# A chunked state-space scan with a gated feed-forward behind it: block 1 in the order of the later blocks, pair 4 prepared in block 0, the last output in two halves, other dummies

## Chip, cores and metric

The kernel runs on one core of one Trainium2 chip. The metric is the device time of one execution in microseconds (us). Three executions of the kernel before took 128.85, 129.83 and 133.45 us; the median is 129.83.

A core has these engines: PE (TensorE, with its weight loads shown apart as PEld), DVE (VectorE), ACT (ScalarE), POOL (GpSimd) and SP (SyncE, which here only issues DMAs). Each engine works through its own queue in order, and they meet at semaphores.

## What is computed

```python
# x [4, 8, 768, 32], a [4, 8, 768], B and C [4, 8, 768, 16]
for c in range(nc):                       # chunks of 32 tokens
    cum = np.cumsum(log_a[chunk])
    L = np.exp(cum_i - cum_j) * causal
    M = (C_c @ B_c.T) * L
    y[chunk] = M @ x_c + (C_c @ state) * np.exp(cum)
    state = np.exp(sum(log_a)) * state + sum_j B_j x_j * np.exp(cum_end - cum_j)
t = y.transpose(0, 2, 1, 3).reshape(3072, 256)
out = (np.maximum(t @ w_gate, 0) * (t @ w_val)) @ w_out   # w_gate, w_val [256, 1536], w_out [1536, 256]
```

## The kernel before

**Tiling.** The scan uses chunks of 128 tokens instead of 32. Two chunks (256 tokens) of all 8 heads are a pair; there are 12 pairs, 3 to each of the 4 batches. Pairs 0 to 3 (`NWIDE`) have B and C loaded with two neighbouring tokens side by side in a partition, the others token by token. The decays are folded into B and C: C is multiplied and B divided by the running product of `a`, so that what is left is a masked C B^T. The feed-forward runs in 6 blocks of 512 tokens, two pairs each. The output of the scan, `yT` (256 features by tokens, bf16), is its input.

**Steps of a pair.** `load` brings B, C and x in by SP's queue (`held` does the same behind a tiny DVE memset, which keeps the DMAs from starting earlier). `scale` is `scale_bc` (two multiplications that give the scaled B and C, the tile `bs`) and `to_x` (x to bf16, the tile `xb`), on POOL for the pairs from 2 on. `turn` transposes B and C on PE; `tevac` copies them out (ACT and DVE). `G` is the masked product's eight matmuls; `gevac` brings them to `gs` with the mask: one and a half of four quarters by ACT with two selects on POOL behind it (`causal`, L168), the rest by DVE. `states` (`state` for the first batch) adds to the running state in PSUM, `spread` (`sevac`) copies it to `Sm` on DVE. `inter` (state times C) and `Dm` (`gs` times x) write the bank `y`, and `yevac` copies it to `yT`: in two strided copies for pairs 0 to 3, in one for the others.

**Steps of a block b.** For each of 12 slices f of 128 hidden features, `gv` makes gate and value for all 512 tokens: two matmuls of 512 columns each (L526, L529), a Relu on ACT (L532) and a product on DVE (L533). `gvh` does the same for half the tokens (256 columns; L544, L551, L552). `fout` makes 128 tokens of output with 12 matmuls of 256 columns (L564), and `foevac` copies and stores: for two groups at a time on ACT and SP; in the last block one at a time, by ACT and ACT's DMA queue for even groups, by DVE and SP's queue for odd ones.

**The order.** `in_order` ties every engine to the order in which the program names its instructions, so the order is written by hand. In block b the names are P = 2b + 2 and Q = 2b + 3, the two pairs of the next block, and W = 2b + 1, the second pair of this block. The first `nh` slices are done in halves: first the half whose `yT` comes from pair 2b, then, when W's `yT` is there, the other. `nh` is 4 in block 0 (whose first halves stand ahead of the loop), 6 in block 1 and 5 after that. W's `inter` and `Dm` come after f == 4 in block 1, after f == 2 in the later blocks. In the later blocks `states(P)` follows them directly; in block 1 it comes behind `fout(1, 0)`. The prologue, up to L689, works through pairs 0 and 1; `keep_warm(n, cols)` puts n matmuls without use (dummies, tile `w`, L200) into PE's queue there.

PSUM has five shared banks (`bank`) that rotate through gate, value, `o` and `g`, and one bank each for `y`, the transposes and the state.

Of the kernel before, what the change touches and what calls it, by code (L numbers as in the profile page):

```python
# [8 lines left out]
FP32 = mybir.dt.float32  # L9
# [20 lines left out]
def kernel(  # L30
# [13 lines left out]
    nc = tc.nc  # L44

    NB, NH, S, D = x.shape
# [5 lines left out]
    NF = DF // 128  # L52
# [13 lines left out]
    def bank(name="bank", shape=(128, 512), dtype=FP32):  # L66
        return mm.tile(list(shape), dtype, tag="shared", bufs=NSHARED, name=name)
# [129 lines left out]
    def keep_warm(n, cols=512):  # L197
        w = mm.tile([128, 512], FP32, tag="y", name="w")
        for _ in range(n):
            nc.tensor.matmul(out=w[:, 0:cols], lhsT=warm[:, 0:128], rhs=warm[:, 0:cols],  # L200
                             start=True, stop=True)
# [73 lines left out]
    def scale_bc(p, eng, js=slice(0, 2), f=None):  # L275
        b, c0, _ = place(p)
        src, dst = views(p, js)
        if f is None:
            if p < NWIDE:
                f = wfac[:, p, js].rearrange("s j r h -> s (j r) h")  # L280
            else:
                f = fac[:, b, c0:c0 + 2].rearrange("s c j h -> s (c j) h")
        n = f.shape[1]
        for t in range(2):
            eng.tensor_tensor(  # L285
                out=dst[:, :, t], in0=src[:, :, t],
                in1=f[:, :, 4 * t:4 * t + 4].to_broadcast([128, n, 4, N]), op=ALU.mult)

    def to_x(p, eng, f=None):
        xb = att.tile([128, 2 * NH * D], BF16, tag="xb", name="xb", bufs=6)  # L290
        xr = st[p]["xr"].rearrange("s i h d -> s (i h) d")
        out = xb.rearrange("s (k d) -> s k d", d=D)
        if f is None:
            copy(eng, out, xr)
        else:
            eng.tensor_tensor(out=out, in0=xr, in1=f.to_broadcast([128, 2 * NH, D]),
                              op=ALU.mult)
        st[p]["x"] = [xb[:, i * NH * D:(i + 1) * NH * D] for i in range(2)]

    def scale(p, eng):  # L300
        new_bs(p)
        scale_bc(p, eng)
        to_x(p, eng)
# [65 lines left out]
    def G(p):  # L369
        s = st[p]  # L370
        if "gp" not in s:
            G_banks(p)
        g = s["gp"]
        for i in range(2):
            for q in range(4):
                r = slice(32 * q, 32 * q + 32)
                nc.tensor.matmul(  # L377
                    out=split(p, g[q][:, i]), lhsT=s["BT"][r, i], rhs=ct(p, i, r),
                    start=(i == 0), stop=True, tile_position=(32 * q, 0),
                    skip_group_check=True)  # L380
        s["gs"] = att.tile([128, 4, 4, 128], BF16, tag="gs", name="gs", bufs=2)
# [51 lines left out]
    def states(p):  # L433
        c0 = 2 * (p % PPB)
        last = c0 + 2 == NC
        chunks[p] = (st[p]["B"], st[p]["x"])
        todo = [(0, p, 0)]
        if c0:
            todo.insert(0, (0, p - 1, 1))
        if not last:  # L440
            todo += [(1, p, 0), (1, p, 1)]
        for n, (k, e, i) in enumerate(todo):
            B_, x_ = chunks[e]
            xi = x_[i].rearrange("s (t q d) -> s q t d", t=2, q=4)
            for q in range(4):
                nc.tensor.matmul(  # L446
                    out=A_ps[0][32 * q:32 * q + 32, 0, 64 * k:64 * k + 64].rearrange(
                        "p (t d) -> p t d", t=2),
                    lhsT=B_[i][:, 32 * q:32 * q + 32], rhs=xi[:, q],
                    start=(n == 0 and c0 == 0), stop=True, tile_position=(0, 32 * q),  # L450
                    skip_group_check=True)

    def spread(p):
        for k in range(1 if 2 * (p % PPB) + 2 == NC else 2):
            S[2 * p + k + 1] = n = att.tile([128, 2, 128], BF16, tag="Sm", name="Sm", bufs=5)
            a = A_ps[0][:, 0, 64 * k:64 * k + 64].rearrange("p (t o d) -> p t o d", t=2, o=1)
            nc.vector.tensor_tensor(  # L457
                out=n.rearrange("p t (q d) -> p t q d", q=4),
                in0=a.to_broadcast([128, 2, 4, D]),
                in1=smask.rearrange("p t (q d) -> p t q d", q=4), op=ALU.mult)  # L460
# [58 lines left out]
    fst = {}  # L519
# [39 lines left out]
    def fout(b, ts):  # L559
# [3 lines left out]
        for f in range(NF):  # L563
# [2 lines left out]
                rhs=wo[:, f], start=(f == 0), stop=(f == NF - 1),  # L566
                skip_group_check=True)

    def foevac(b, ts):
        last = b == NBLK - 1  # L570
        if ts % 2 == 0 and not last:
            return
        ob = ffn.tile([128, 2, DM], FP32, tag="ob", name="ob", bufs=3)
        r0 = b * 512 + ts * 128
        if last:
            i = ts % 2
            (nc.vector.tensor_copy if i else nc.scalar.copy)(out=ob[:, i], in_=fst["o"][:, i])
            (nc.sync if i else nc.scalar).dma_start(out=out[r0:r0 + 128, :], in_=ob[:, i])
            return
        nc.scalar.copy(out=ob, in_=fst["o"])  # L580
        nc.sync.dma_start(
            out=out[r0 - 128:r0 + 128, :].rearrange("(i p) m -> p i m", p=128), in_=ob)
# [9 lines left out]
    nc.vector.reciprocal(r0, d0)  # L592
    scale_bc(0, nc.vector, B_, r0)
    transp(0, 1, True)
    keep_warm(4, 128)
    transp(0, 0, True)
    cevac(0, nc.scalar)
    bevac(0, nc.vector)
# [3 lines left out]
    nc.vector.reciprocal(wfac[:, 1, 0], d1)  # L602
    new_bs(1)
    scale_bc(1, nc.vector, C_)
    G(0)
    gevac(0)

# [18 lines left out]
    keep_warm(3)  # L626
    astep(0, 0)
    sevac(0, 0)
    keep_warm(9, 128)
    scale_bc(1, nc.gpsimd, B_)  # L630
    cast_x(1, (1,))
    weights(4, 8, (1,))
# [58 lines left out]
    for b in range(NBLK):  # L691
        P, Q, W = 2 * b + 2, 2 * b + 3, 2 * b + 1
        more = P < NPAIR
        for n in (P + 2, P + 3):
            if b and n < NPAIR:
                load(n, nc.sync)

        nh = (4, 6, 5)[min(b, 2)]
        for f in range(nh):
            if b == 0:  # L700
                continue
            gvh(b, f, 0)
            if b and f == (4 if b == 1 else 2):
                inter(W, 0)
                inter(W, 1)
                Dm(W)
                if b > 1 and more:
                    states(P)
                yevac(W, nc.scalar)
                if b > 1 and more:  # L710
                    spread(P)
        for f in range(nh):
            gvh(b, f, 1)
            if b == 1 and f in (0, 3):
                scale(P if f == 0 else Q, nc.gpsimd)
        for f in range(nh, NF):
            gv(b, f)
            if b == 0:
                if f == 5:
                    turn(P)  # L720
                    tevac(P, nc.scalar, nc.vector)
                    scale_bc(Q, nc.gpsimd)
                if f == 7:
                    back(P)
                    backevac(P, nc.vector)
                if f == 8:
                    held(Q, bc=False)
                    held(Q + 1)
                if f == 9:
                    state(P, 0)  # L730
                if f == 10:
                    state(P, 1)
                    held(Q + 2)
                    turn(Q)
                    tevac(Q, nc.scalar, nc.vector)
            elif more:
                if f == (6 if b == 1 else 5):
                    turn(P)
                    tevac(P, nc.scalar, nc.vector)
                    if b > 1:  # L740
                        scale(Q, nc.gpsimd)
                if f == (9 if b == 1 else 8):
                    turn(Q)
                    tevac(Q, nc.scalar, nc.vector)
                    if Q + 1 < NPAIR:
                        scale(Q + 1, nc.gpsimd)
        if more and b != 1:
            inter(P, 0)
            inter(P, 1)
        fout(b, 0)  # L750
        foevac(b, 0)
        if b == 1:
            states(P)
        if more:
            G(P)
        if b == 1:
            spread(P)
        if more:
            gevac(P)
        if b == 0:  # L760
            to_x(Q, nc.gpsimd)
            back(Q)
            backevac(Q, nc.vector)
        fout(b, 1)
        foevac(b, 1)
        if b == 0:
            for n in range(NB):
                nc.vector.reciprocal(fac[:, n, :, 0], fac[:, n, :, 1])
        fout(b, 2)
        foevac(b, 2)  # L770
        if more:
            if b == 1:
                inter(P, 0)
                inter(P, 1)
            Dm(P)
            states(Q)
            yevac(P, nc.scalar)
            G(Q)
            spread(Q)
            gevac(Q)  # L780
        fout(b, 3)
        foevac(b, 3)

    in_order(tc)

# [29 lines left out]
```

## Time and profile before

| | |
|---|---|
| runs shown | 128.85, 129.83, 133.45 us (median 129.83) |
| profiled execution | 128.56 us |
| its span, first to last instruction | 126.9 us |
| mean granted clock of PE | 0.986 |
| DMA | 11.72 MB; under 512 B: 66912 of 73136 packets |

| engine | busiest groups (line: count, mean ns of one) |
|---|---|
| PE | L564 `o`: 288, 273; L526 and L529 `gate`, `val`: 84 each, 379; L544 `gv`: 240, 273 |
| PEld | L564: 288, 98 |
| DVE | L533 `h`: 42, 686; L552 `h`: 60, 421; L398 `gs`: 24, 684 |
| ACT | L532 `r`: 42, 597; L551 `r`: 60, 385; L389 `gs`: 12, 590 |
| POOL | L285 `bs`: 16, 620; L168 `gs`: 12 of 644 and 12 of 409; L259 `xb`: 9, 609 |

The mean of one matmul has its way through the array in it and overlaps with its neighbours; in the chain of waits, where each counts from start to start, one of 256 columns takes 0.109 us and one of 512 takes 0.216. "Released by" and idle times are inferred from semaphores.

### The profile page before, as it was taken

To read this page: it belongs to the slowest core of one execution; us is meant where nothing else is said; L and a number is where in the kernel's file an instruction comes from. 1 tells how busy PE (TensorE), PEld (TensorE's weight loads), DVE (VectorE), ACT (ScalarE), POOL (GpSimd) and SP (SyncE) were. 2 spreads that over 40 slices of the span, in tenths; PEclk is the share of its full clock that TensorE was granted. 3 is DMA by queue.
4 is the path that set the end of the run, shared out by engine and by line. 5 is a ranking of instruction groups with operands and counts; after the bars stand their busy time and mean duration, and the time that the engine had idled before them with its cause. 6 is when DMAs were issued, how large, how long until landed. Compare 5 with 4: busy or idle time off the path is not lost.

```text
span 126.9 us, 3376 instructions
## 1 busy us (share of the span) xinstructions
PE 120.6 (95%) x1261; PEld 83.5 (66%) x1261; DVE 93.5 (74%) x225; ACT 78.1 (62%) x173; POOL 42.4 (33%) x79
## 2 busy tenths in 40 slices
PE   6789999999999999999999999999999999999980
PEld 2337784568876568884577875577874678854860
DVE  5686988869969875898865888865898756787420
ACT  4062677644888734888745787635987446877310
POOL 7959696005651313703112803132600033000000
PEclk9967999999999999999999999999999999999999
DMA  3999999979998987099742288822200002200031
GB/s 65 145 184 184 154 204 144 156 109 107 103 178 151 122 88 154 33 121 121 75 71 83 90 79 118 97 47 83 83 5 0 0 0 88 83 0 0 5 123 42
DMA packets 73136, 11.72 MB, mean 92 GB/s; under 512 B 66912, under 2 KB 73120, under 8 KB 73120
## 3 DMA queue, kind: packets, MB, share of 16 engines
q1 hardware_dynamic: 61328, 8.23, 42.0%
q0 software_dynamic: 9424, 2.75, 20.8%
q10 hardware_dynamic: 2368, 0.52, 2.2%
q8 instruction: 10, 0.16, 0.5%
q14 instruction: 6, 0.05, 0.1%
HBM read 11.11 MB, written 3.15 MB: 112 GB/s over the span
## 4 chain that ended last, share of the span: by engine, by line
PE 91%; DVE 3%; DMA 2%; issue 1%; ACT 0%; DVEq 0%
PE o L564 26%; PE gv L544 22%; PE val L529 14%; PE gate L526 14%; PE g L377 3%; PE y L500 3%; DMA a_sb<-in_a_dram 2%; PE y L489 2%; PE tp L317 2%; PE w L200 2%; PE d L222 1%; DVE cp L207 1%; PE A_ps L446 1%; PE bt L358 1%; DVE bs L285 1%; PE A_ps L240 1%
## 5 line engine op out<-in xcount | busy, mean ns | idle before, releaser
L564 PE MATMUL o<-wo,h 128*128 128x256 bf16 x288 | 34.1, 273 | 0.0
L533 DVE TENSOR_TENSOR h<-r,val 128x512 bf16<-128x512 bf16 x42 | 28.8, 686 | 5.4 <-ACT r L532 2.2
L564 PEld LDWEIGHTS <-h 128*128 128x128 bf16 x288 | 27.2, 98 | 5.4 <-issue 1.9
L532 ACT ACTIVATE r<-gate 128x512 bf16<-128x512 f32 x42 | 25.1, 597 | 8.0 <-PE gate L526 7.1
L552 DVE TENSOR_TENSOR h<-r,gv 128x256 bf16<-128x256 bf16 x60 | 24.9, 421 | 5.5 <-ACT r L551 4.8
L168 POOL TENSOR_SCALAR_AFFINE_SELECT gs<-gs 128x512 bf16<-128x512 bf16 (+1 forms) x24 | 12.1, 527 | 46.7 <-ACT gs L389 46.7
L551 ACT ACTIVATE r<-gv 128x256 bf16<-128x256 f32 x60 | 23.1, 385 | 3.3 <-PE gv L544 0.9
L526 PE MATMUL gate<-yT,wg 128*128 128x512 bf16 x84 | 25.0, 379 | 0.0
L529 PE MATMUL val<-yT,wv 128*128 128x512 bf16 x84 | 25.0, 379 | 0.0
L544 PE MATMUL gv<-yT,wg 128*128 128x256 bf16 x120 | 23.1, 273 | 0.2
L544 PE MATMUL gv<-yT,wv 128*128 128x256 bf16 x120 | 22.9, 273 | 0.0
L398 DVE TENSOR_TENSOR gs<-g,masks 128x512 bf16<-128x512 f32 x24 | 15.4, 684 | 4.3 <-PE g L377 4.2
L529 PEld LDWEIGHTS <-wv 128*128 128x128 bf16 x84 | 8.2, 98 | 9.9
L285 POOL TENSOR_TENSOR bs<-bcr,fac 128x256 bf16<-128x256 f32 x16 | 9.6, 620 | 13.4 <-DMA bcr<-in_B_dram 13.4
L389 ACT CAST gs<-g 128x512 bf16<-128x512 f32 x12 | 7.1, 590 | 9.6 <-PE g L377 9.6
L259 ACT CAST yT<-y 128x512 bf16<-128x512 f32 (+1 forms) x14 | 7.1, 528 | 9.3 <-PE y L500 3.6
L544 PEld LDWEIGHTS <-wv 128*128 128x128 bf16 x120 | 11.7, 98 | 1.6 <-issue 0.2
L544 PEld LDWEIGHTS <-wg 128*128 128x128 bf16 x120 | 11.2, 98 | 2.1 <-issue 0.4
L526 PEld LDWEIGHTS <-wg 128*128 128x128 bf16 x84 | 7.8, 98 | 5.9
L457 DVE TENSOR_TENSOR Sm<-A_ps,smask 128x256 bf16<-128x256 f32 x15 | 5.8, 419 | 6.6 <-PE A_ps L446 6.5
L580 ACT COPY ob<-o 128x512 f32<-128x512 f32 x10 | 5.8, 585 | 4.8 <-PE o L564 4.8
L200 PE MATMUL w<-warm 128*128 128x128 bf16 (+1 forms) x30 | 6.7, 380 | 1.3 <-DVE first L118 1.3
(79 smaller groups left out, 104.5 us busy)
## 6 DMA issues: line engine op xcount, KB each, us to landing
out_dram<-ob SPq DMA_DIRECT2D x10, 256.0 KB, 2.2
xr<-in_x_dram SPq DMA_DIRECT2D x18, 128.0 KB, 3.3
bcr<-in_C_dram SPq DMA_DIRECT2D x16, 64.0 KB, 3.0
bcr<-in_B_dram SPq DMA_DIRECT2D x16, 64.0 KB, 3.0
wg<-in_moe_w_gate_dram POOLq DMA_DIRECT2D x3, 256.0 KB, 5.5
wv<-in_moe_w_val_dram POOLq DMA_DIRECT2D x3, 256.0 KB, 5.6
wo<-in_moe_w_out_dram POOLq DMA_DIRECT2D x1, 768.0 KB, 8.5
bcr<-in_B_dram SPq DMA_DIRECT2D x4, 128.0 KB, 4.6
```

Of the source, the lines that this page charges most:

```text
L168: nc.gpsimd.affine_select(out=dst, in_=dst, pattern=pattern, compare_op=ALU.is_ge, fill=0.0, base=0, channel_multiplier=-1)
L200: nc.tensor.matmul(out=w[:, 0:cols], lhsT=warm[:, 0:128], rhs=warm[:, 0:cols], start=True, stop=True)
L285: eng.tensor_tensor(out=dst[:, :, t], in0=src[:, :, t], in1=f[:, :, 4 * t:4 * t + 4].to_broadcast([128, n, 4, N]), op=ALU.mult)
L398: nc.vector.tensor_tensor(out=d[:, q], in0=g[q], in1=m, op=ALU.mult)
L526: nc.tensor.matmul(out=g, lhsT=wg[:, k, fs], rhs=yT[:, k, tk], start=(k == 0), stop=(k == 1))
L529: nc.tensor.matmul(out=v, lhsT=wv[:, k, fs], rhs=yT[:, k, tk], start=(k == 0), stop=(k == 1))
L532: nc.scalar.activation(r, g, AF.Relu)
L533: nc.vector.tensor_tensor(out=fst[b][:, f], in0=r, in1=v, op=ALU.mult)
L544: nc.tensor.matmul(out=gv_[:, j], lhsT=w[:, k, fs], rhs=yT[:, k, tk], start=(k == 0), stop=(k == 1), skip_group_check=True)
L551: nc.scalar.activation(r, gv_[:, 0], AF.Relu)
L552: nc.vector.tensor_tensor(out=fst[b][:, f, u * 256:(u + 1) * 256], in0=r, in1=gv_[:, 1], op=ALU.mult)
L564: nc.tensor.matmul(out=o[:, ts % 2], lhsT=fst[b][:, f, ts * 128:(ts + 1) * 128], rhs=wo[:, f], start=(f == 0), stop=(f == NF - 1), skip_gr ...
```

## The change

Block 1 takes the order of the later blocks: five slices in halves, W after f == 2, `states(P)` and `spread(P)` behind W, the turns at f == 5 and f == 8, `inter(P)` ahead of `fout(1, 0)`. For that, pair 4 (Q + 1 of block 0) is scaled in block 0: `scale_bc` on POOL ahead of pair 3's selects, `to_x` behind them, the loads one slice earlier, the reciprocals of the decays earlier and without the first batch, which nothing reads. The last 128 tokens of output are made by `fout_last` in two column halves, the first copied and stored by ACT, the second by DVE and SP. Dummies: 5 instead of 4 between the two transposes of pair 0, two new ones ahead of `G(0)`, 6 instead of 9 ahead of `Dm(0)`.

```diff
+    def fout_last(b):
+
+        r0 = b * 512 + 384
+        for m in range(2):
+            ms = slice(m * 128, (m + 1) * 128)
+            o = bank("o", (128, 128))
+            for f in range(NF):
+                nc.tensor.matmul(out=o, lhsT=fst[b][:, f, 384:512], rhs=wo[:, f, ms],
+                                 start=(f == 0), stop=(f == NF - 1))
+            ob = ffn.tile([128, 128], FP32, tag="obl", name="ob", bufs=2)
+            (nc.vector.tensor_copy if m else nc.scalar.copy)(out=ob, in_=o)
+            (nc.sync if m else nc.scalar).dma_start(out=out[r0:r0 + 128, ms], in_=ob)
...
     transp(0, 1, True)
-    keep_warm(4, 128)
+    keep_warm(5, 128)
     transp(0, 0, True)
...
     scale_bc(1, nc.vector, C_)
+    keep_warm(2, 128)
     G(0)
...
     sevac(0, 0)
-    keep_warm(9, 128)
+    keep_warm(6, 128)
     scale_bc(1, nc.gpsimd, B_)
...
-        nh = (4, 6, 5)[min(b, 2)]
+        nh = 5 if b else 4
         for f in range(nh):
             if b == 0:
                 continue
             gvh(b, f, 0)
-            if b and f == (4 if b == 1 else 2):
+            if f == 2:
                 inter(W, 0)
                 inter(W, 1)
                 Dm(W)
-                if b > 1 and more:
+                if more:
                     states(P)
                 yevac(W, nc.scalar)
-                if b > 1 and more:
+                if more:
                     spread(P)
         for f in range(nh):
             gvh(b, f, 1)
-            if b == 1 and f in (0, 3):
-                scale(P if f == 0 else Q, nc.gpsimd)
         for f in range(nh, NF):
             gv(b, f)
...
                     backevac(P, nc.vector)
-                if f == 8:
                     held(Q, bc=False)
                     held(Q + 1)
...
             elif more:
-                if f == (6 if b == 1 else 5):
+                if f == 5:
                     turn(P)
                     tevac(P, nc.scalar, nc.vector)
-                    if b > 1:
-                        scale(Q, nc.gpsimd)
-                if f == (9 if b == 1 else 8):
+                    scale(Q, nc.gpsimd)
+                if f == 8:
                     turn(Q)
                     tevac(Q, nc.scalar, nc.vector)
                     if Q + 1 < NPAIR:
                         scale(Q + 1, nc.gpsimd)
-        if more and b != 1:
+        if more:
             inter(P, 0)
             inter(P, 1)
         fout(b, 0)
         foevac(b, 0)
-        if b == 1:
-            states(P)
+        if b == 0:
+            for n in range(1, NB):
+                nc.vector.reciprocal(fac[:, n, :, 0], fac[:, n, :, 1])
         if more:
             G(P)
-        if b == 1:
-            spread(P)
-        if more:
             gevac(P)
         if b == 0:
             to_x(Q, nc.gpsimd)
+            new_bs(Q + 1)
+            scale_bc(Q + 1, nc.gpsimd)
             back(Q)
             backevac(Q, nc.vector)
         fout(b, 1)
         foevac(b, 1)
-        if b == 0:
-            for n in range(NB):
-                nc.vector.reciprocal(fac[:, n, :, 0], fac[:, n, :, 1])
         fout(b, 2)
         foevac(b, 2)
         if more:
-            if b == 1:
-                inter(P, 0)
-                inter(P, 1)
             Dm(P)
             states(Q)
             yevac(P, nc.scalar)
             G(Q)
             spread(Q)
             gevac(Q)
-        fout(b, 3)
-        foevac(b, 3)
+            if b == 0:
+                to_x(Q + 1, nc.gpsimd)
+            fout(b, 3)
+            foevac(b, 3)
+        else:
+            fout_last(b)
```

## The prediction

> **What bounds the kernel now.** I read the page first, then the chain of waits in order of time, then busy time and clock by stretch, and last the timelines of POOL and SP.
>
> ```profile
> span 126.9 us, 3376 instructions
> ...
> PE 120.6 (95%) x1261; PEld 83.5 (66%) x1261; DVE 93.5 (74%) x225; ACT 78.1 (62%) x173; POOL 42.4 (33%) x79
> ...
> PEclk9967999999999999999999999999999999999999
> ```
>
> TensorE is busy for 95% of the span, and after the first quarter of a slice row its digits are all 9: from 8.6 us to 123.3 us the chain of waits runs almost wholly on PE. So work on another engine matters only where it makes PE wait, and there are few such places. PEclk shows one weak stretch, slices 3 and 4. The chain of waits there (start, length, what):
>
> ```profile
> 6.85 0.30 PE tpb L317 x2
> 7.17 0.44 DVE BT L259
> 7.66 0.61 PE g L377 x8
> ...
> 8.60 1.28 PE w L200 x3
> 9.88 0.21 PE A_ps L415
> 10.09 0.91 PE w L200 x9
> 11.04 0.41 PE y L500 x16
> ...
> 11.65 0.45 ACT yT L259
> ```
>
> The reader sees dummies (w, L200) on the path: three wide ones cost 1.28 us, 0.43 each, though 512 columns take 0.216 in the later stages (gate L526, 0.43 for two). The clock is half. Busy time by stretch, cut at steps of 3.41 us (the last columns are clock, DMA share, GB/s):
>
> ```profile
> 3.97:7.38 3.41, 2.40 (x33) 1.43 (x30) 2.40 (x9) 0.84 (x2) 3.33 (x7) 1.00 2.04 141
> 7.38:10.79 3.41, 3.24 (x27) 1.75 (x24) 2.87 (x10) 1.31 (x4) 2.00 (x6) 0.50 1.56 190
> 10.79:14.20 3.41, 3.21 (x49) 2.18 (x46) 2.28 (x7) 1.81 (x5) 2.22 (x3) 1.00 1.41 152
> ```
>
> The granted clock is 0.50 for exactly one stretch of 3.41 us, after a stretch with PE busy for 2.40 of 3.41. Block 1 in the chain of waits:
>
> ```profile
> 33.30 2.18 PE gv L544 x20
> 35.48 0.11 PE y L489 x2
> 35.59 0.34 PE y L500 x16
> 35.93 0.54 PE gv L544 x4
> ...
> 36.48 0.27 PE gv L544
> ...
> 36.79 2.67 PE gv L544 x23
> 39.46 0.43 PE gate L526 x2
> ```
>
> Here 48 narrow matmuls should take 48 x 0.109 = 5.24 (12 take 1.31 at 52.05), with 0.45 for the two y groups 5.69; they take 39.46 - 33.30 = 6.16. PE stalls for 0.47 us. The same count for block 2 (52.05 to 57.17: 40 x 0.109 + 0.22 + 0.34 + 0.09 = 5.01 of 5.12) leaves 0.11. The end:
>
> ```profile
> 118.01 5.25 PE o L564 x48
> ...
> 123.34 0.42 DVE ob L577
> ```
>
> **The change part by part.**
>
> *Dummies.* Three narrow ones less before Dm(0). At half clock one takes 0.107 (0.91 for nine is a mix: half clock to 10.79, then 0.055). Six take 6 x 0.107 = 0.64, so Dm(0) can start 0.27 earlier, at 10.77. What is late next: its gs are done at 9.99 (POOL) and 10.06 (DVE), Sm for inter at 10.56, so nothing holds it. One dummy more at 6.5 lies in PE's idle 0.19 before 6.85, where PE waits for DVE's bs; without that cover it costs 0.06. The two before G(0) lie in the idle 0.17 before 7.66, where PE waits for DVE's BT. They take 0.11 at full and 0.21 at half clock, so 0 to 0.04 sticks out, 0.21 if BT were early. I take -0.24; bounds -0.31 and 0.
>
> *Block 0.* Two memsets of 0.06 move one step up on DVE, from 24.37 to 23.65, into the slack before the next h; SP's x load for pair 3 and all loads for pair 4 go out 0.7 earlier, and pair 5's behind them. Three reciprocals (four took 1.38, so 1.04) move ahead of gs(2) into DVE's idle 1.00 before 28.39; gs(2) may end 0.05 later, at 30.06, and Dm(2) runs at 31.13, so the price is nothing, and without that idle 1.04 would eat all but 0.1 of this margin. The fourth is gone. POOL gets scale_bc(4) (two, 1.20) ahead of gevac(3)'s two selects, and to_x(4) (0.61) behind them. Queued behind scale_bc(4) is Dm(3), through the selects. B(4)'s second half is issued at about 28.5 - 0.7 = 27.7 and loads of that stretch land in 2.9 to 3.4, so it lands by 31.2. POOL is free from to_x(3) at 30.6; scaling ends at 32.4, the selects start at 32.8 as now, to_x(4) ends at 34.4. It is wanted by states(4) after Dm(3), at about 35.0. Zero, with 0.4 to spare on the one and 0.6 on the other.
>
> *Block 1.* Six half steps per side become five: eight narrow matmuls become four wide ones, 8 x 0.109 against 4 x 0.216, nothing. Dm(3) runs after three half steps, at 33.30 + 1.31 + 0.11 = 34.7; gs(3) ends at 33.83 on POOL and 33.93 on DVE. ACT then copies yT in two pieces (0.76, at 35.98 now) while PE has states(4) 0.09 and two half steps 0.87 to do; now it has only one, and there it stalls. So the stall should shrink to block 2's 0.11; but block 2's yT copy is 0.59, so 0.17 may remain on top. Gain 0.19 to 0.36, I take 0.33. POOL's scale(5), now placed after turn(4), still starts when its load lands (36.30, 38.80 in the trace) and is wanted by turn(5) beyond 42: nothing. The inter and states moved over from the end of the block are the same instructions on PE.
>
> *Last output.* Twelve matmuls of 256 columns (1.31) become 24 of 128, each with its own weight load. No long run of this kind is in the trace. The nearest rows: four transposes with four weight loads 0.22, four inter matmuls 0.22, so 0.055 each, 1.32 in all: nothing. The far bound is the mean weight load of 98 ns: 24 x 0.098 = 2.35, 1.04 worse. I take the row of four, as there too each matmul has a fresh weight. A page speaks against this part: the Trainium skill, "TensorE: Matmul & The Clock Gate", section "Back-to-back issue gap", gives about 81 ns per matmul for a stream of load and matmul at 128 columns; by that estimate the 24 would take 1.94, 0.6 more. The groups of four here disagree with it. After PE, DVE copies 128 columns instead of 256: 0.42 becomes 0.29 by the 128x128 products on DVE (L285), and the last DMA is half as large; its 128 KB moved in about 0.5 us. But the first half leaves on ACT's queue right behind the DMA of 122.38, and lands 2.3 after its issue at about 123.05, 125.35, where SP's 1.7 now gives 123.80 + 1.7 = 125.5. So -0.15 to -0.35; I take -0.2.
>
> Sum: -0.24 - 0.33 - 0.2 = -0.77 against the profiled 128.56, whose span is 126.9 with 1.66 around it: 127.8. The three runs shown (128.85, 129.83, 133.45) all lie above it; the two lower ones by 0.78 on average. So I expect **128.5** as the median, 1.0% under 129.83.
>
> **The rivals.**
>
> *The clock stays whole (25%).* If the added dummies lift the stretch before 7.38 over what the gate asks, the half-clock stretch goes. G(0) then takes 0.34 (as at 13.18) instead of 0.61, DVE's gs end at 9.8 and Sm at 10.3, and inter ends at 10.4 instead of 11.63: 1.2 earlier, 0.95 beyond my sum. What may take it back is wo: issued at 17.64, 8.5 to landing, so in place at 26.14, and wanted at 26.49. If it does not move, only 0.35 of the shift survives. 0.1 to 0.95 more gain: 127.5 to 128.4 on the median, 126.8 with a lucky one. For: the gate changed at a step of 3.41 us, and three dummies are added ahead or at its edge. Against: one of them adds 0.06 to 2.40.
>
> *The gate closes later (11%, the slower one).* With three dummies fewer, or with the earlier stretch at full clock and thus sooner done, PE waits more in 7.38 to 10.79, and the half clock falls on 10.79 to 14.20, where PE is busy for 3.21 of 3.41 with real work. That costs half of it, 1.6: 130.1, slower than before. It decides when that stretch's busy time falls toward the 2.40 that closed the gate; by my sum it stays above 3.0, which speaks against it. Two such stretches would give 131.7. The Trainium skill, the same page, section "Part 1: The HAM clock gate", lets the clock fall only after an idle window of about 3.4 us; by that this rival could not happen. The trace agrees on the length, 3.41, but the stretch before the fall was busy for 2.40, so I leave the rival its chance.
>
> *POOL holds block 1 back (6%).* If B(4) lands after 34.7 - 1.03 - 1.20 = 32.5, 4.8 after its issue, PE waits at Dm(3). With the longest landing of the run from such loads, 7.4, scaling ends at 36.3, the selects at 37.3: 2.6 lost, and the 0.33: 131.4. Against: 2.9 to 3.4 in that stretch.
>
> *The last 24 matmuls go at the pace of weight loads (8%).* With 98 ns for each, +1.04: 129.5, no gain that shows. For: no run of more than six in the trace. Against: the groups of four, and six dummies at 5.48 whose six weight loads span 0.34. (The Trainium skill's 81 ns, from the page and section named above, would give 129.1.)
>
> *It does not do what it says (13%).* The stall of block 1 is carried by ACT's backlog, not the order, and the dummies' time reappears as a wait for gs: only the tail is left, 129.3.
>
> **How the numbers follow.** The forecast as worked out has 37%, its own range 127.6 to 129.3. A difference under 2% (2.6 us) cannot be told from none in these runs. Below 127.2 lie part of the whole-clock case and the forecast with a lucky median: 0.6 x 25% + 0.2 x 37% = 22%. Above 132.4 lie two half-clock stretches or a run like 133.45: 8%. The range 126.7 to 130.2 takes in all cases but the POOL one and the tails.
>
> **What would show it.** Right: Dm(0) near 10.8; block 1's half steps in 5.1 + 0.1 with Dm(3) at 34.4 to 34.7; POOL's scale_bc(4) before 32.5 and no wait of PE on gs or bs; 24 last matmuls in 1.3, a DVE copy of 0.29. Wrong: a clock of 0.5 after 10.8, a POOL wait on B(4) that ends past 32.5, PE idle before o at 26 (wo), or last matmuls 0.08 or more apart.

## The result, and the profile after

| | before | changed |
|---|---|---|
| executions | 20 | 20 |
| median, us | 129.01 | 127.78 |
| lowest to highest | 128.53 to 133.45 | 127.47 to 128.88 |
| profiled execution / its span | 128.56 / 126.9 | 127.47 / 125.8 |

The ratio of the times is 0.991 (95% interval 0.989 to 0.994): 0.9% faster. A second set of the changed kernel, nine executions, gave 0.993 (0.989 to 0.997). The ratios leave out executions more than 1.5% above the fastest of their kernel, among them the 133.45 us here and, below, one of 133.46 us (dummies alone) and one of 309.23 us (block 1 alone), whose causes are not known.

The page of the changed kernel:

```profile
span 125.8 us, 3385 instructions
...
PE 119.7 (95%) x1262; PEld 83.2 (66%) x1269; DVE 92.9 (74%) x223; ACT 78.3 (62%) x173; POOL 42.5 (34%) x79
...
PEclk9967999999999999999999999999999999999999
```

Nothing has changed in kind: PE is as busy as it was, and the dip of PEclk is still there. The chain of waits in the prologue (start, length, what):

```profile
9.85 0.21 PE A_ps L415
10.06 0.66 PE w L200 x6
10.76 0.47 PE y L500 x9
...
11.43 0.46 ACT yT L259
11.93 1.03 PE gv L544 x8
```

Dm(0) (y, L500) starts at 10.76 instead of 11.04, the first half step at 11.93 instead of 12.14. Busy time by stretch (the third column from the right is the granted clock):

```profile
3.97:7.38 3.41, 2.57 (x34) 1.50 (x31) 2.40 (x9) 0.84 (x2) 3.33 (x7) 1.00 1.99 137
7.38:10.79 3.41, 3.13 (x28) 1.57 (x30) 2.83 (x10) 1.31 (x4) 2.04 (x6) 0.52 1.56 191
```

The first stretch goes from 2.40 to 2.57, in part by the one added dummy that lies in it, in part because the eight wide dummies at the start end 0.08 later; the clock falls all the same. Block 1 in the chain of waits:

```profile
33.08 1.31 PE gv L544 x12
34.39 0.11 PE y L489 x2
34.50 0.34 PE y L500 x16
34.84 0.12 PE A_ps L446 x16
34.96 3.16 PE gv L544 x28
...
51.34 1.31 PE gv L544 x12
```

Two later lines of the chain of before:

```profile
46.40 0.23 PE A_ps L446 x16
...
52.05 1.31 PE gv L544 x12
```

The 40 narrow matmuls now run with 0.1 of stall (3.16 for 28, where 28 x 0.109 is 3.05), and the block takes 51.34 - 33.08 = 18.26 us, against 52.05 - 33.30 = 18.75 before. Where the stall was, ACT's timelines show, first that of before, then that of the changed kernel:

```profile
35.98 0.76 ACT L259 CAST yT<-y 128x256 bf16<-128x256 f32 x2
```

```profile
34.89 0.76 ACT L259 CAST yT<-y 128x256 bf16<-128x256 f32 x2
```

Before, the two pieces of the copy to yT take 0.45 each and end at 36.43 and 36.74. PE's first matmul of the second halves, which reads the first piece, starts at 36.48, and the next, which reads the second, at 36.79: both wait for ACT. Now the copy ends at 35.65, while PE still has two half steps of first halves to do, up to 34.96 + 0.87 = 35.83. POOL's timeline around the end of block 0:

```profile
29.80 0.61 POOL L259 CAST xb<-xr 128x512 bf16<-128x512 f32 x1
31.32 1.20 POOL L285 TENSOR_TENSOR bs<-bcr,fac 128x256 bf16<-128x256 f32 x2 [0.91 <-DMA bcr<-in_B_dram]
32.58 1.04 POOL L168 TENSOR_SCALAR_AFFINE_SELECT gs<-gs 128x512 bf16<-128x512 bf16 x2
33.56 0.61 POOL L259 CAST xb<-xr 128x512 bf16<-128x512 f32 x1
```

The scaling of pair 4 (second line) waits 0.91 for its B, ends at 32.52, and the selects of pair 3 follow it at once, with no idle time between. They are not late by it: they start 0.07 after ACT's first `gs` (32.51), as they did before (32.80 after 32.73). The timeline at the end:

```profile
121.07 1.50 PE L576 MATMUL o<-wo,h 128*128 128x128 bf16 x24
...
122.07 0.27 ACT L579 COPY ob<-o 128x128 f32<-128x128 f32 x1 [0.43 <-PE o L576]
122.37 0.34 ACTq L580 DMA_DIRECT2D out_dram<-ob  x1
122.61 0.29 DVE L579 COPY ob<-o 128x128 f32<-128x128 f32 x1 [2.23 <-PE o L576]
122.92 0.34 SPq L580 DMA_DIRECT2D out_dram<-ob  x1
```

In the chain of waits, where each matmul counts from start to start, the last 24 take 1.35:

```profile
117.30 3.93 PE o L564 x36
121.23 1.35 PE o L576 x24
```

From the first o matmul of the last block to the end of the span it takes 125.8 - 117.30 = 8.50, against 126.9 - 118.01 = 8.89 before.

So the profiled executions differ thus: 0.22 by the start of the first o matmuls (26.43 against 26.65), 0.49 in block 1, nothing in blocks 2 to 5 (65.96 in both, from 51.34 to 117.30 and from 52.05 to 118.01), 0.39 at the end. That is 1.10, as the spans say.

### The profile page after: what moved, and what is told of

It reads as the page before. It is cut to its first block, busy times and chain, and to the rows that moved or that the text cites. A ratio compares the mean times of both kernels' runs of the same rounds, so it can differ in the third digit from the quotient of the medians.

```text
span 125.8 us, 3385 instructions
## 1 busy us (share of the span) xinstructions
PE 119.7 (95%) x1262; PEld 83.2 (66%) x1269; DVE 92.9 (74%) x223; ACT 78.3 (62%) x173; POOL 42.5 (34%) x79
## 4 chain that ended last, share of the span: by engine, by line
PE 92%; DVE 2%; DMA 2%; issue 1%; ACT 0%
PE o L564 25%; PE gv L544 21%; PE val L529 16%; PE gate L526 14%; PE g L377 3%; PE y L500 3%; DMA a_sb<-in_a_dram 2%; PE y L489 2%; PE tp L317 2%; PE w L200 2%; PE d L222 1%; PE o L576 1%; DVE cp L207 1%; PE bt L358 1%; DVE bs L285 1%
## 5 line engine op out<-in xcount | busy, mean ns | idle before, releaser
L533 DVE TENSOR_TENSOR h<-r,val 128x512 bf16<-128x512 bf16 x43 | 29.4, 685 | 5.6 <-ACT r L532 2.5
L564 PE MATMUL o<-wo,h 128*128 128x256 bf16 x276 | 32.8, 273 | 0.0
L532 ACT ACTIVATE r<-gate 128x512 bf16<-128x512 f32 x43 | 25.7, 597 | 8.3 <-PE gate L526 7.4
L564 PEld LDWEIGHTS <-h 128*128 128x128 bf16 x276 | 26.0, 98 | 4.9 <-issue 1.9
L552 DVE TENSOR_TENSOR h<-r,gv 128x256 bf16<-128x256 bf16 x58 | 24.0, 420 | 4.6 <-ACT r L551 3.9
L529 PE MATMUL val<-yT,wv 128*128 128x512 bf16 x86 | 25.6, 379 | 0.3
L526 PE MATMUL gate<-yT,wg 128*128 128x512 bf16 x80 | 24.3, 379 | 0.0
L551 ACT ACTIVATE r<-gv 128x256 bf16<-128x256 f32 x58 | 22.3, 385 | 2.9 <-PE gv L544 0.6
L544 PE MATMUL gv<-yT,wg 128*128 128x256 bf16 x116 | 22.2, 273 | 0.1
L544 PE MATMUL gv<-yT,wv 128*128 128x256 bf16 x116 | 22.1, 273 | 0.0
```

Of the source, the lines that this page charges most:

```text
L526: nc.tensor.matmul(out=g, lhsT=wg[:, k, fs], rhs=yT[:, k, tk], start=(k == 0), stop=(k == 1))
L529: nc.tensor.matmul(out=v, lhsT=wv[:, k, fs], rhs=yT[:, k, tk], start=(k == 0), stop=(k == 1))
L532: nc.scalar.activation(r, g, AF.Relu)
L533: nc.vector.tensor_tensor(out=fst[b][:, f], in0=r, in1=v, op=ALU.mult)
L544: nc.tensor.matmul(out=gv_[:, j], lhsT=w[:, k, fs], rhs=yT[:, k, tk], start=(k == 0), stop=(k == 1), skip_group_check=True)
L551: nc.scalar.activation(r, gv_[:, 0], AF.Relu)
```

## The experiments

**The three parts, each alone in the kernel before.**

Dummies alone:

```diff
-    keep_warm(4, 128)
+    keep_warm(5, 128)
...
+    keep_warm(2, 128)
     G(0)
...
-    keep_warm(9, 128)
+    keep_warm(6, 128)
```

> Before with the new counts of dummies alone (5, 2 and 6). If three dummies fewer at half clock are what counts, Dm(0) starts near 10.76 instead of 11.04 and the time falls by 0.2 to 0.25 us, with the half-clock stretch 7.4 to 10.8 still there where the profiled execution has it. If the added dummies keep the clock whole, the 0.50 in that stretch is gone and up to 1.0 us goes. If the three removed ones only uncover a wait for gs or Sm, the first gv stays at 12.1 and nothing is gained.

Ratio 1.004 (1.000 to 1.007): nothing gained, if not a little lost. The profiled execution shows where. Busy time by stretch, and the chain of waits:

```profile
7.38:10.79 3.41, 3.41 (x30) 1.74 (x29) 2.73 (x10) 1.56 (x5) 1.34 (x4) 1.00 1.55 190
```

```profile
8.04 0.33 PE w L200 x2
8.36 0.59 PE g L377 x6
...
11.31 5.97 DMA xb<-in_x_dram
17.28 0.04 issue
17.33 0.35 PE y L500 x12
```

The recorded clock is 1.00, but PE is at half speed: in the timeline the three wide dummies behind G(0) start at 9.03 and the next matmul at 10.31, so they take 1.28, 0.43 each. In this execution PE was never at full speed before about 10.5. Here the two added dummies are not hidden: G(0) starts at 8.36. In the execution profiled for the last output alone, also at half speed but with the old dummies, it starts at 7.94. Then the selects on POOL and, behind them, the load of the second half of pair 1's x go out later (11.31 against 10.93), and Dm(1) waits for it until 17.33 (15.83 there). Of these 1.50 the later issue explains 0.38; the rest is the load itself, under way for 5.97 instead of 4.86, and no run shows why. Where PE is at full speed by 5 us, as in the profiles of before and after, the same edit seems to pay. All six profiled executions with a recorded mean clock of 0.986 or 0.987 start in that way; I call those like executions. Here two of them lie at 128.43 and 128.47; seven of before, run beside these, have a median of 128.70, but lie between 128.45 and 129.16.

Last output alone (`fout_last` in place of `fout(5, 3)` and `foevac(5, 3)`):

> Before with the last 128 tokens of output in two column halves alone. If the halves pay by a shorter last copy and a smaller last DMA, the last 24 matmuls take 1.35 us, DVE's copy 0.29 and the time from the first o matmul of the last block to the end of the span falls by 0.4 (8.89 to 8.5). If only the copy counts, 0.13. If the weight loads pace the matmuls at 98 ns, they take 2.35 and the kernel is 0.6 slower.

Ratio 0.999 (0.996 to 1.002). The end in its chain of waits:

```profile
118.12 3.93 PE o L564 x36
122.05 1.35 PE o L576 x24
...
123.43 0.29 DVE ob L579
```

The 24 matmuls take 1.35, the copy 0.29, and the end 126.6 - 118.12 = 8.48: the 0.4 is there in the profile. But 0.4 of 129 is 0.3%, no more than the half width of the interval, so the times by themselves do not show it (medians 128.52 and 128.90).

Block 1 alone, with pair 4 prepared in block 0. It is the changed kernel with 4, 0 and 9 dummies, as before, and

```diff
-            fout_last(b)
+            fout(b, 3)
+            foevac(b, 3)
```

> Before with block 1 in the later blocks' order and pair 4 prepared in block 0, dummies and last output as before. If the order made the stall, block 1 (first half step to first half step of block 2) takes 18.26 instead of 18.75 us, and the time falls by 0.5. If the stall was ACT's backlog or what came of a slightly earlier start, it stays within 0.1 of 18.75 here and the gain of the changed kernel came from elsewhere.

Ratio 0.996 (0.994 to 0.999). Its chain of waits:

```profile
33.27 1.31 PE gv L544 x12
...
35.14 3.16 PE gv L544 x28
...
51.53 1.31 PE gv L544 x12
```

Block 1 takes 51.53 - 33.27 = 18.26. The order made the stall.

In the like executions the parts give 0.25, 0.35 and 0.61 under 128.70 (medians 128.45, 128.35 and 128.09; two, four and four executions); together 1.2, where the whole change has 1.08 (127.62, six executions of the first set). So there they roughly add up, though like executions of before have medians of 128.58 and 128.56 beside the later runs, so that each of these differences is uncertain by 0.1 or more. The ratios over all executions do not add up (+0.4, -0.1 and -0.4%, together -0.1%, against -0.9%). The gap, 0.7%, is a little more than the four intervals together allow (about 0.6%), and what makes it was not settled.

**Pair 4 scaled in block 1.**

```diff
-            new_bs(Q + 1)
-            scale_bc(Q + 1, nc.gpsimd)
...
         nh = 5 if b else 4
+        if b == 1:
+            scale(P, nc.gpsimd)
...
-            if b == 0:
-                to_x(Q + 1, nc.gpsimd)
```

> The changed kernel, but pair 4 is scaled and its x made bf16 at the top of block 1, so on POOL behind pair 3's selects; the loads stay early. If the preparation in block 0 is what lets block 1 run in this order, scale_bc(4) runs at 33.6 to 34.8 and to_x(4) to 35.4, states(4) is wanted at 34.84, PE waits there about 0.6 us, and 0.4 to 0.6 of the gain goes (block 1 at 18.7 to 18.9). If ACT's yT copy is the later one anyway (35.65), PE loses the wait at states but gets it back at the second halves, and under 0.2 goes.

Ratio 1.001 (0.997 to 1.004). The three executions with a mean clock of 0.986 or 0.987 have a median of 128.19, 0.57 above the changed kernel's 127.62, as the first theory has it; the others go up to 129.59, and the one of them that was profiled starts at half speed. PE's timeline in block 1 (idle time before, and what ended it, in brackets):

```profile
35.48 0.41 PE L500 MATMUL y<-gs,xb 128*32 128x128 bf16 x16
35.71 0.20 PE L446 MATMUL A_ps<-xb,bx 128*32 128x64 bf16 x4
36.43 0.27 PE L446 MATMUL A_ps<-xb,bs 128*32 128x64 bf16 x12 [0.51 <-POOL xb L259]
```

The first four matmuls of states(4) use pair 3 and run; the twelve that need pair 4 wait for POOL's bf16 x. The second theory falls: the wait stands at states and is not given back. From `inter` (35.27 in PE's timeline, 34.23 in the changed kernel) to the first half step of block 2 (53.08 and 51.34 in the chains of waits) it takes 17.81 instead of 17.11, 0.70 more. Without the preparation in block 0, the new order is worth nothing.

**The last output in quarters** (four column quarters of 64, ACT and DVE in turn):

```diff
-        for m in range(2):
-            ms = slice(m * 128, (m + 1) * 128)
+        for m in range(4):
+            ms = slice(m * 64, (m + 1) * 64)
```

> The changed kernel with the last 128 tokens in four column quarters: 48 matmuls of 64 columns, each with its own 128x128 weight load. If columns pace the last matmuls, 48 take about 48 x 0.028 = 1.35 us, as the 24 do, and the shorter last copy gives 0.05. If a matmul with a fresh weight load cannot go below about 0.05 (what the 24 show is then both limits at once), they take 2.4 to 2.6 and the kernel is 1.0 to 1.2 slower than the changed one.

```profile
122.13 1.56 PE L576 MATMUL o<-wo,h 128*128 128x64 bf16 x48
```

48 matmuls, each with a full weight load, in 1.56 with the last one's way through the array (0.19): 0.029 each. Columns set the pace here (0.056 for 128 columns, 0.029 for 64); the 98 ns of a weight load's row are no pace. The end takes 126.9 - 118.37 = 8.53, so quarters give nothing over halves, and the 0.05 hoped for did not come: in the chain of waits ACT's copies and DMA issues (0.22 and 0.35 each) now follow one another. The ratio, 0.998 (0.996 to 1.000), is above the changed kernel's. The profiled execution starts its last o matmuls 1.07 later than the changed kernel's (118.37 against 117.30), so in it the difference came from ahead of them: it started at half speed. None of the ten is a like execution, and why is open, since the edit is at the other end of the kernel.

**Six dummies instead of nine, none added** (one line of the kernel before):

> Before with nine dummies cut to six ahead of Dm(0), none added elsewhere. Theory: the three removed pay (0.2 to 0.3 in every execution), and the three added ones cost where PE is still at half clock, so this one gains 0.2 to 0.3 on the median where all new dummies together gained nothing. Rival: fewer dummies lose as much by a later clock, and this one too stays within 0.1 of before.

Ratio 1.001 (0.998 to 1.004): a miss. In its profile the first half step starts at 11.86, 0.28 sooner than before, with a span 0.2 shorter; over all executions it does not show, and three like executions lie only 0.10 under seven of before (medians 128.48 and 128.58). Not all of the 0.28 is the edit's either: the clock fell 0.7 later in this profile, at about 8.07, and that is ahead of the place that was edited. So the added dummies alone do not explain why the dummies as a whole gained nothing.

**The stretch before 7.38 filled** (changed kernel):

```diff
     keep_warm(8)
+    keep_warm(6, 128)
...
-    keep_warm(6, 128)
+    keep_warm(11, 128)
     scale_bc(0, nc.vector, C_, d0)
...
-    keep_warm(5, 128)
+    keep_warm(10, 128)
```

> The changed kernel with 16 more narrow dummies in the stretch 3.97 to 7.38: 6 behind the eight wide ones, 11 instead of 6 behind the first decay matmuls, 10 instead of 5 between the transposes. If the half clock after 7.38 follows from too little work in that stretch, the recorded 0.50 is gone where PE was at full clock by 5, G(0) takes 0.34, and such executions gain 0.3 to 0.9. Where PE is still at half clock, each costs 0.107 and up to 1.7 is lost. The median tells which is more frequent: below 127.5 the one, above 128.3 the other.

Median 127.74 of six, between the two bounds, ratio 0.992 (0.989 to 0.995), as the changed kernel. But the clock did stay whole in the profiled execution: nine tenths of PEclk throughout, G(0) in 0.39, Dm(0) at 10.11. PE's timeline shows what became of that:

```profile
14.73 0.24 PE L501 MATMUL y<-gs,xb 128*32 128x128 bf16 x4
16.09 0.35 PE L501 MATMUL y<-gs,xb 128*32 128x128 bf16 x12 [1.11 <-DMA xb<-in_x_dram]
```

Dm(1) reaches pair 1's second x 1.11 before it lands (issued at 10.61, 5.43 under way) and starts its main part at 16.09; in the changed kernel all of it starts at 15.52. There the load went out at 10.63, no earlier and no later, and took 4.5. So in this execution the whole clock gained nothing, because the load took longer; why it did is not shown.

**Few dummies** (changed kernel, twice):

```diff
-    keep_warm(6, 128)
+    keep_warm(2, 128)
     scale_bc(0, nc.vector, C_, d0)
...
-    keep_warm(5, 128)
+    keep_warm(1, 128)
...
-    keep_warm(2, 128)
     G(0)
...
-    keep_warm(6, 128)
+    keep_warm(2, 128)
     scale_bc(1, nc.gpsimd, B_)
```

> The changed kernel with few narrow dummies: 2 instead of 6 behind the first decay matmuls, 1 instead of 5 between the transposes, none ahead of G(0), 2 instead of 6 ahead of Dm(0). Theory: dummies only cost where PE is at half clock early, so the executions above 128.2 lose 0.4 to 0.8 us of their time, the others 0.2 (Dm(0) at 10.4 to 10.6), median 127.2 to 127.5. Rival: the dummies are what brings the full clock back at 10.8; without them it comes 3.41 later, real work runs at half speed up to 14.2, and 0.5 to 1.6 is lost.

> The changed kernel with few narrow dummies once more, for more executions of it. If few dummies free it of the slow group, none lies above 128.0, as the five so far (127.2 to 127.4); if those five were chance, about a third does.

Ratios 0.988 (0.986 to 0.991; five executions) and 0.986 (0.981 to 0.991; six). The median of the eleven is 127.29, of the changed kernel's 29 executions 127.81. Three of the eleven lie above 127.5, up to 129.04, so the five first were chance in that respect. This is the lowest median measured; that it beats the changed kernel is not shown, as the intervals still overlap. In the first profile Dm(0) starts at 10.07 and the first half step at 11.63, but little of that reaches the end. PE's timeline:

```profile
26.26 1.47 PE L564 MATMUL o<-wo,h 128*128 128x256 bf16 x12 [0.29 <-DMA wo<-in_moe_w_out_dram]
```

The first o matmuls wait for wo, which lands 9.3 after its issue (8.5 in the changed kernel). The second profile, at 128.34, is one of half speed, up to 13.8.

**Loads in another order.** Pair 1's second x right behind its first (changed kernel); and, with few dummies, that and wo's load ahead of pair 2's x:

```diff
-    cast_x(1, (0,))
+    cast_x(1)
...
-    cast_x(1, (1,))
```

```diff
-    cast_x(2)
     weights_out(0, NF)
+    cast_x(2)
```

> The changed kernel with the second chunk of pair 1's x loaded right behind the first, ahead of the gate weights 4 to 8, not behind the scaling of pair 1's B on POOL. Theory: in the executions above 128.2, where PE is at half clock up to 9 or later, Dm(1) waits for this load (issue 10.9 to 11.3, landing 4.9 to 6.0 later), so they lose 0.4 to 1.2 us of their time and the spread of the executions narrows, the lower ones near 127.6 stay. Median 127.4 to 127.7. Rival: the executions differ by the clock alone, and both groups stay where they are; or the load only pushes the weights behind it, and a later wait takes its place.

> Few narrow dummies (2, 1, 0, 2) and pair 1's second chunk early as in the two runs of these parts, and wo's load issued ahead of pair 2's x. Theory: the few dummies bring the first gv to 11.6 and wo's wait of 0.29 at 26 goes too, so 0.3 to 0.5 under few dummies alone: 126.8 to 127.0, or 1.5% under before. Rival: pair 2's x or a scaling of pair 2 or 3 becomes the late one, and it stays at 127.2 or above.

The first: six executions at 126.7 (two), 127.6 and 128.7 to 128.8 (three), median 128.11. The spread did not narrow, as the theory had it. The ratio 0.984 (0.978 to 0.990) rests on the lower three, and I read no gain from it. The lowest times of all kernels are among them; but its profiled execution, at 128.8, waits elsewhere in the chain, as the second rival had it:

```profile
18.31 9.24 DMA wo<-in_moe_w_out_dram
27.55 0.04 issue
27.59 1.47 PE o L564 x12
```

The second: 128.22 to 130.72 in twelve executions, median 128.65, ratio 0.998 (0.995 to 1.002). The rival held, in the chain of its profile:

```profile
16.22 8.71 DMA xb<-in_x_dram
24.93 0.04 issue
24.97 0.27 PE A_ps L415
```

Pair 2's x became the late one: 8.7 to its landing, against at most 6.3 with few dummies alone, and the first o matmuls start at 27.41. In these profiles each of three loads (x of pair 1, x of pair 2, wo) is once the last to land; moving one ahead made another late.

**The changed kernel once more**, beside these:

> The changed kernel once more, beside the others on the same chip: 127.4 to 128.9, median 127.8.

127.46 to 129.27, median 128.27, 0.5 above the first set. Its profiled execution is one of half speed: busy time and clock by stretch, and the wide dummies in the chain of waits:

```profile
7.38:10.79 3.41, 3.41 (x28) 1.78 (x28) 2.72 (x10) 1.52 (x5) 1.40 (x4) 1.00 1.56 192
```

```profile
9.19 1.28 PE w L200 x3
```

Recorded 1.00, and 0.43 for 512 columns.

## Why the prediction was right, and where it was not

The direction and the range held, and the size came close (1.0% forecast, 0.9% measured). That closeness is luck in part. The forecast drop, from 129.83 to 128.5, is 1.33 us, but only 0.77 of it are terms of the change; the rest comes from setting the forecast against the mean of two executions and the kernel before against the median of three. Terms that were too small and a median that was too high cancel. That no difference under 2% could be told was too cautious: 20 executions of each give an interval of 0.25% to either side. By its steps:

*Dummies, -0.24.* Right for executions like the one it was worked out from: Dm(0) at 10.76 (10.77 forecast; agreement to 0.01 is chance, since the half-clock stretch lay 0.16 later), 0.22 at the first o matmuls. Wrong as a forecast for all: it took the profiled clock for that of every execution. In seven other profiles PE runs at half speed from the start to between 9.5 and 13.8, and the covers named for the three added dummies are gone; that price (0.21 for the two ahead of G(0)) was written down, but as a case that would not come. Alone the dummies gained nothing.

*Block 0, nothing.* Right, with less to spare. The scaling of pair 4 ended at 32.5 (32.4 forecast), the selects started at 32.58, so 0.06 was left of the 0.4; to_x(4) ended at 34.2, 0.67 ahead of states(4). B(4)'s second half went out only 0.2 earlier than before, at 28.3, not 0.7, and landed by 31.2 because it took 2.9, the lower end of what was allowed for. Taking the preparation away showed what it carries: 0.5 of idle PE at states(4) and a block longer by 0.70 in the trace, 0.57 in like executions.

*Block 1, -0.33.* The mechanism was right, the term too small: 0.49. The stall shrank to block 2's own, 0.47 to 0.11 (the longer yT copy cost nothing more), and states(4), which took 0.23 on PE behind `fout(1, 0)`, takes 0.12 where it is now. I had counted it as the same instructions and so as nothing; why they take less there is not shown.

*Last output, -0.2.* The mechanism was right, the term too small: 0.39. The 24 matmuls take 1.35 (1.32 forecast). The limit that I set, ACT's half landing 2.3 after its issue, was a misreading: 2.3 is the middle of ACT's two stores of 128 KB, and the last of them, at 122.38, landed after 1.7, as SP's does; the 2.8 belongs to the one at 119.8. Those of 64 KB land 1.5 after their issue on both queues. So DVE's half alone sets the end: its copy is 0.13 shorter and its store 0.2, together 0.33 of the 0.39.

*From the profiled execution to the median, +0.78.* This is the step that was most off in size. Two of three executions set it; over 20 the medians lie 0.45 (before) and 0.31 (changed) above the profiled ones. With the terms 0.3 too small, it put the forecast 0.7 above the 127.78 measured.

*The rivals.* A whole clock did not come by this change; where it was brought about with more dummies, it was paid back to a load, as that rival's second half had it, though to x of pair 1 and not to wo (wo was the one with few dummies). The half clock on later work did appear, though not as that rival had it. Mostly it was a start at half speed that lasts. In three profiles (six dummies alone, few dummies, few dummies with other loads) the fall itself came later, at 8.05 to 8.2 instead of 7.38, and Dm(0) ran at half speed in 0.61 or 0.62 instead of 0.41; but it was a shift of 0.7 or 0.8, not of a whole stretch, and no 1.6 was lost. POOL did not hold block 1 back. The weight loads did not pace the last matmuls: both the halves and the quarters disagree with 98 ns as a pace; the trace has 56 ns for 128 columns. The Trainium skill's page "TensorE: Matmul & The Clock Gate", section "Back-to-back issue gap", gives 81 ns for 128 columns, and the trace does not agree with that either.

## What to carry to other kernels

Where PE is the bound, count what each stage's matmuls should take and compare with what the chain of waits says; a stage that is slower than its neighbours of the same make shows a stall, and moving its neighbours' order onto it, with the data it then needs prepared ahead, was worth about that difference here (0.36 of stall, and 0.11 at states). A prologue's gain must be checked in several executions, since the clock it starts with differs between them, and followed to the first place where loads decide. Dummies that hide at full clock can sit on the path at half.

## What was not expected of the hardware

The granted clock in the rows can be wrong at the start. Seven of the profiled executions (dummies alone, last output alone, pair 4 late, quarters, the changed kernel again, few dummies again, pair 1's x early) record 1.00 throughout the prologue, while 128 columns take 0.107 and 512 take 0.43 us until between 9.5 and 13.8 us; the rows of before do the same up to 4 us (eight wide dummies in 3.22, recorded 1.00). It is consistent with a clock that is recorded only from its first change on.

The clock fell after a stretch in which PE was busy for 2.40 of 3.41 us, and again after 2.57. The Trainium skill, page "TensorE: Matmul & The Clock Gate", section "Part 1: The HAM clock gate", puts the fall behind an idle window; by the busy time of the rows these stretches were not idle, so the trace does not agree. With 16 more narrow dummies (3.35) it did not fall. When it rises does not follow from the busy time of the rows either: in the profile of the changed kernel once more PE stayed at half speed through 7.38 to 10.79, which the rows call busy for 3.41 of 3.41, and on to about 12.7. What the clock does follow is open. The length of the half-clock stretch, 3.41 us, agrees with the window that the Trainium skill gives in the same section.

In the prologue half of pair 1's x takes 4.0 to 6.0 us from issue to landing and wo 7.9 to 9.3, from profile to profile, even of the same kernel (wo 8.5 and 8.0 in the two of the changed kernel). At the end a store of 64 KB lands 0.2 us sooner than the last ones of 128 KB (1.5 against 1.7).
